# Three small moves in a kernel bound by TensorE: an earlier weight load with a later transpose, later first scores, and one mix on another engine

## Chip, cores, metric

One core of a Trainium2 chip. The metric is the device time of one execution in microseconds (us); medians of several executions are quoted. All comparisons are between fast-state runs, except where a run is called slow.

## The reference, cut to what matters

```python
# attention without softmax: 8 batches, 3008 rows, 256 columns, z has 64 columns
scores = (1 / S) * z @ z.T
attn   = maximum(scores, 0) ** 2
x      = u * (attn @ v)
# then for all 24064 rows, with w_in 256x2048 and w_out 2048x256
h   = x @ w_in
out = (h * cos(h)) @ w_out
```

## The kernel before: the parts that matter here

The work is cut into 48 columns of 512 rows (448 in the last column of each batch). Column s has a phase A (value matmuls, with scores for later columns in between) and a phase B (products with `w_in` and, two columns later, with `w_out`). From column 1 on the product with `w_out` is done from sums of parts ("mixes"), for which four mixed weights (`w_mix`) are made once. The order of every engine's instructions is the order in which the code emits them. GpSimd issues the loads that change type; SyncE issues the transposes, which are DMAs too.

To read the traces: matmul results land in PSUM, used here as pairs of banks E (scores, products with `w_in`) and single banks M. ScalarE takes a score's relu into r and the cosine into c. VectorE squares r into A, makes g = h * cos(h) and the sums sm of the value matmuls, and the later mixes s2 and s4. GpSimd makes s1, the early mixes. x is the sums times uT, the transposed u; the code calls that transpose the "turn" of u. A tiles are transposed too, and are written again when they are free.

```python
upool = pool("u", 2)                      # TWO buffers for u, shared by all columns

def load_u(s):                            # issued on GpSimd's queue
    t = upool.tile([P, 4, D], FP16, name="u16")
    load_rows(t, u, s // NC, s % NC)
    u16s[s] = t

def turn_u(s):                            # a transposing DMA, issued on SyncE's queue
    t = upool.tile([P, 8, P], FP16, name="uT")
    nc.sync.dma_start_transpose(t, u16s.pop(s).rearrange("p j d -> p (j d)"))
    uTs[s] = t

def phase_a_first(s, n, extra={}):        # phase A of columns 0, 1 and 2
    # ... (n scores spread over steps lo..hi)
    for i in range(n):
        p = lo + (hi - lo) * i // (n - 1)
        at[p] = at.get(p, 0) + 1
    for i, (dh, k) in enumerate(steps):
        # ... (two value matmuls, "a pair", per step)
        if dh > 0 and (k % 4 == 3):
            drop_piece((b, J, k // 4))
            if s > 0:
                emit_turns((0, 0), 1)     # one A transpose
                if k < 4:
                    turn_u(s)
                elif k < 8:
                    for d in range(2):
                        gate_mul(s - 1, d, late_sums.pop(0))
        for _ in range(at.get(i, 0)):
            emit_score(later=squares if s == 0 and i == lo else None)
    # ...
    hold(late_sums[0][0:1, 0:1])          # GpSimd waits here for the column's sums
    load_u(s + 1)

def mix_early(m, j):                      # on GpSimd
    # ...
    nc.gpsimd.tensor_tensor(s1[:, f, 0:n], g[:, f, low], g[:, lower, low], ALU.add)
    nc.gpsimd.tensor_tensor(g[:, f, low], g[:, f, up], g[:, f, low], ALU.subtract)

# main sequence
phase_a_first(1, 12)
nc.gpsimd.dma_start(w_out16, moe_w_out.rearrange("(k p) f -> p k f", p=P))
for i in range(2):
    emit_h(0, i)()
phase_a_first(2, 14)                      # ends with load_u(3)
emit_turns((0, 3))
turn_u(3)
load_u(4)                                 # GpSimd: the fifth u
load_z(1, 0)
mix_weights()                             # GpSimd: the four mixed weights
phase_b(2)                                # GpSimd: x of column 2, then the first mixes
```

Of the kernel before, what the change touches and what calls it, by code (L numbers as in the profile page):

```python
# [14 lines left out]
def kernel(  # L15
# [9 lines left out]
    nc = tc.nc  # L25
    AF = mybir.ActivationFunctionType
    ALU = mybir.AluOpType
# [4 lines left out]
    P = 128  # L32
# [6 lines left out]
    NSLOT = B * NC  # L39
# [26 lines left out]
    w_out16 = kpool.tile([P, NFT, D], FP16, name="w_out16")  # L66
    w_mix = kpool.tile([P, 4, NFT // 2, P], FP16, name="w_mix")
    s1, s2, s4 = (kpool.tile([P, NFT // 2, 2 * P], FP16, name=n) for n in ("s1", "s2", "s4"))
# [25 lines left out]
    def drop_piece(key):  # L94
        i = pieces.pop(key)
        if pending.get(i):
            pending[i] = "dropped"
        else:
            free_pieces.append(i)
# [46 lines left out]
    def load_rows(t, src, b, g):  # L146
        full = 4 if g < NC - 1 else 3
        nc.gpsimd.dma_start(
            t[:, 0:full, :],
            group_rows(src[b], g),  # L150
        )
        if full == 3:
            for r in range(2):
                nc.gpsimd.dma_start(t[r * H:(r + 1) * H, 3, :], src[b, S - H:S, :])
# [6 lines left out]
    def load_u(s):  # L161
# [4 lines that stand above are left out]
    def turn_u(s):  # L166
# [3 lines that stand above are left out]
# [64 lines left out]
    def emit_turns(due, more=0):  # L234
        while turns and (turns[0][0] <= due or more > 0):
            if turns[0][0] > due:
                more -= 1
            (b, c), key = turns.pop(0)
            b, J, I = key
            i = turn_slots[key]  # L240
            a = piece_bufs[i]
            if I == J:
                a4 = a.rearrange("p (k w) -> p k w", w=CW)
                for rr in range(1, 4):
                    rows = P if J * 4 + rr < NB - 1 else H
                    nc.sync.dma_start_transpose(
                        a4[:, 0:rr, rr * P:rr * P + rows],
                        a[0:rows, rr * CW:rr * CW + rr * P],
                    )
            else:  # L250
                d = new_piece((b, I, J))
                nc.sync.dma_start_transpose(d.rearrange("p (n j) -> p n j", j=P), a)
            if pending.pop(i) == "dropped":
                free_pieces.append(i)
# [10 lines left out]
    def emit_value(b, J, k, t, dh, bank, start, stop):  # L265
        nc.tensor.matmul(  # L266
            bank[:, 0:width(J)],
            vs[b, k // 4][t * H:(t + 1) * H, k % 4, dh * P:(dh + 1) * P],
            value_rhs(b, J, k, t),
            start=start,  # L270
            stop=stop,
        )
# [8 lines left out]
    def gate_mul(s, dh, sm, eng=None):  # L281
        eng = eng or nc.vector
        J = s % NC
        b = s // NC
        W = width(J)
        if s not in xs:
            if J == NC - 1 and b % 2 == 1:
                xs[s] = xodd
            else:
                xs[s] = xpool.tile([P, 2, CW], FP16, name="x")  # L290
        x = xs[s]
        uT = uTs[s].rearrange("p (k d) j -> p k d j", d=2)
        nk = W // P
        eng.tensor_tensor(  # L294
            x[:, dh, 0:nk * P].rearrange("p (k j) -> p k j", j=P),
            sm[:, 0:nk * P].rearrange("p (k j) -> p k j", j=P),
            uT[:, 0:nk, dh, :],
            ALU.mult,
        )
        if nk < 4:  # L300
            dst = x[:, dh, nk * P:W] if b % 2 == 1 else xodd[:, dh, W:CW]
            eng.tensor_tensor(
                dst, sm[:, nk * P:W], uT[:, nk, dh, 0:W - nk * P], ALU.mult
            )
# [47 lines left out]
    def hold(src):  # L352
        nc.gpsimd.tensor_copy(mark[:, 0:1], src)

    def phase_a_first(s, n, extra={}):
        b, J = s // NC, s % NC
        ea = e_order.pop(0)
        pair = [E[ea][:, 0, :], E[ea][:, 1, :]]
        acc = [pair, M] if s == 1 else [M, pair]
        last = NB - 1  # L360
        run = 1 if s == 0 else 2
        steps = [
            (dh, k)
            for I in range(0, NC, run)
            for dh in range(2)
            for k in range(4 * I, min(4 * (I + run), last))
        ] + [(2, last)]
        lo, hi = 5 if s == 0 else 2, 42
        at = {}
        for i in range(n):  # L370
            p = lo + (hi - lo) * i // (n - 1)
            at[p] = at.get(p, 0) + 1
        for i, (dh, k) in enumerate(steps):
            if i in extra:
                extra[i]()
            if dh == 2:
                emit_value(b, J, last, 0, 0, acc[0][0], False, True)
                emit_value(b, J, last, 1, 1, acc[1][1], False, True)
            else:
                for t in range(2):  # L380
                    emit_value(
                        b, J, k, t, dh, acc[dh][t], k == 0, k == last - 1 and t != dh
                    )
            if dh > 0 and (k % 4 == 3):
                drop_piece((b, J, k // 4))
                if s > 0:
                    emit_turns((0, 0), 1)
                    if k < 4:
                        turn_u(s)
                    elif k < 8:  # L390
                        for d in range(2):
                            gate_mul(s - 1, d, late_sums.pop(0))
            for _ in range(at.get(i, 0)):
                emit_score(later=squares if s == 0 and i == lo else None)
        if s == 0:
            turn_u(0)
        late_sums.extend(gate_sum(s, *acc[dh]) for dh in range(2))
        hold(late_sums[0][0:1, 0:1])
        load_u(s + 1)
        e_order.append(ea)  # L400

# [31 lines left out]
    def halves_of(m):  # L433
        n = T if mwidth(m) == CW else P
        return n, slice(0, n), slice(T, T + n)

    def mix_early(m, j):
        g, f = gs[m], slice(2 * j, 2 * j + 2)
        n, up, low = halves_of(m)
        lower = slice(F + 2 * j, F + 2 * j + 2)  # L440
        nc.gpsimd.tensor_tensor(s1[:, f, 0:n], g[:, f, low], g[:, lower, low], ALU.add)  # L441
        nc.gpsimd.tensor_tensor(g[:, f, low], g[:, f, up], g[:, f, low], ALU.subtract)  # L442

    def mix_late(m, which, c):
        g, f = gs[m], slice(4 * c, 4 * c + 4)
# [146 lines left out]
    def phase_b(s):  # L592
        y, hs = s - 2, [(s - 1, i) for i in (0, 4, 1, 5, 2, 6, 3, 7)]
        if s == 2:
            hs = [(0, i) for i in range(2, 8)] + hs
        for dh in range(len(late_sums)):
            gate_mul(s, 2 - len(late_sums), late_sums.pop(0), nc.gpsimd)
        if mixed(y):
            late = s == NSLOT
            ys = [  # L600
                lambda n=n, i=i: product(y, n, i)
                for i, n in enumerate((1, 5) + order_y[2:] if late else order_y)
            ]
            if mwidth(y) < CW:
                ys.insert(4, lambda: middle(y))
        else:
            ys = [lambda i=i: emit_y(y, i) for i in range(8)]
            ys[7] = lambda f=ys[7]: (f(), store_y(y))
        n = len(hs)
        if n > 8:  # L610
            after = (1, 2, 4, 5, 7, 8, 10, 11)
        elif s == NSLOT:
            after = (0, 1, 3, 4, 5, 6, 7)
        elif mixed(y):
            after = (0, 1, 2, 3, 4, 5, 6, 6)
        else:
            after = (0, 1, 2, 3, 4, 5, 6, 6)
        for i, (m, unit) in enumerate(hs):
            times_c = emit_h(m, unit)
            if not mixed(y):  # L620
                times_c()
            for f, place in zip(ys, after):
                if place == i:
                    f()
            if mixed(y):
                times_c()
            if s == NSLOT and i in (1, 3):
                for c in range(2):
                    mix_late(y, "s2" if i == 1 else "s4", c)
            if mixed(m) and unit >= 4:  # L630
                mix_early(m, unit - 4)
            if i in (1, 3, 5):
                emit_turns((0, 0), 1)

# [4 lines left out]
    for g in range(NC):  # L639
        eng = nc.sync if g % 2 == 0 else nc.scalar  # L640
# [77 lines left out]

    phase_a_first(0, 12, {4: lambda: turn_late(4), 8: lambda: turn_late(5)})
    phase_a_first(1, 12)  # L720
    nc.gpsimd.dma_start(w_out16, moe_w_out.rearrange("(k p) f -> p k f", p=P))
    for i in range(2):
        emit_h(0, i)()
    phase_a_first(2, 14)
# [65 lines left out]
```

## Time and profile before

| | before |
|---|---|
| median of 5 runs | 1192.74 us (1192.59 to 1193.79) |
| span in the profile | 1191.2 us |
| TensorE busy | 1183.7 us (99%) |
| GpSimd busy | 679.0 us (57%) |

How to read the profile: a row of the timeline gives start, duration, engine, line, operation, output<-input, how many instructions were merged (x16) and, in brackets, how long the engine had stood idle before it and what ended that. The lines that carry the argument are shown in the prediction below.

### The profile page before, as it was taken

How to read it: one execution, taken by the hardware profiler on the slowest of the kernel's cores; microseconds unless marked ns; L12 is line 12 of the kernel's file. 1: busy time of each engine (PE TensorE's matmuls, PEld its weight loads, DVE VectorE, ACT ScalarE, POOL GpSimd, SP SyncE). 2: the span in 40 equal slices, each digit the busy share in tenths (PEclk: the TensorE clock that was granted, in tenths of full speed). 3: DMA queues.
4: the chain of work that ended last, by engine and by line, in shares of the span. 5: the costliest groups of instructions: out<-in, count | busy, mean ns of one | idle time of the engine just before them, and what ended most of it. 6: DMA issues, size and time to landing. Idle time of an engine off the chain costs nothing.

```text
span 1191.2 us, 29044 instructions
## 1 busy us (share of the span) xinstructions
PE 1183.7 (99%) x11887; PEld 726.8 (61%) x11887; DVE 1011.5 (85%) x1302; ACT 794.9 (67%) x927; POOL 679.0 (57%) x717
## 2 busy tenths in 40 slices
PE   9999999999999999999999999999999999999998
PEld 4556665665566656666566665656666566665566
DVE  6888888889988898888988889888888888888776
ACT  7966676667666676667676676666766666666454
POOL 3286745657466573755647556476555655545452
PEclk9999999999999999999999999999999999999999
DMA  9999999569995799955999469984798837974301
GB/s 160 175 172 158 115 171 130 102 122 104 173 127 101 123 137 166 126 89 103 155 152 130 86 106 158 168 123 70 120 162 152 122 72 120 173 122 84 65 20 54
DMA packets 449142, 148.00 MB, mean 124 GB/s; under 512 B 401264, under 2 KB 432496, under 8 KB 449008
## 3 DMA queue, kind: packets, MB, share of 16 engines
q1 hardware_dynamic: 368464, 112.93, 56.6%
q0 software_dynamic: 80032, 32.78, 27.7%
q8 instruction: 93, 1.52, 0.5%
q10 hardware_dynamic: 512, 0.43, 0.1%
q14 instruction: 41, 0.34, 0.1%
HBM read 66.32 MB, written 24.64 MB: 76 GB/s over the span
## 4 chain that ended last, share of the span: by engine, by line
PE 98%; ACT 1%; DVE 1%; issue 0%; POOL 0%; DVEq 0%; ACTq 0%
PE E L412 27%; PE M L490 23%; PE M L266 20%; PE E L266 19%; PE E L202 6%; PE M L533 1%; ACT r L212 1%; PE M L468 1%; DVE g L423 0%; PE E L673 0%; DVE sm L278 0%; PE E L533 0%; POOL s L441 0%; PE M L696 0%; ACT c L420 0%
## 5 line engine op out<-in xcount | busy, mean ns | idle before, releaser
L420 ACT ACTIVATE c<-E 128x1024 f16<-128x1024 f32 (+1 forms) x384 | 385.7, 1007 | 216.4 <-PE E L412 214.1
L423 DVE SCALAR_TENSOR_TENSOR g<-E,c 128x1024 f16<-128x1024 f32 (+1 forms) x384 | 458.9, 1197 | 62.0 <-ACT c L420 60.9
L212 ACT ACTIVATE r<-E 128x512 f16<-128x512 f32 (+1 forms) x342 | 328.0, 967 | 112.3 <-PE E L202 106.6
L266 PEld LDWEIGHTS <-v 64*128 64x128 f16 x4512 | 245.7, 94 | 229.6 <-issue 18.8
L412 PE MATMUL E<-x,w_in 128*128 128x512 f16 (+1 forms) x1408 | 354.0, 375 | 0.0
L441 POOL TENSOR_TENSOR s<-g 128x512 f16<-128x512 f16 (+1 forms) x184 | 207.8, 1130 | 189.3 <-DVE g L423 139.4
L266 PE MATMUL M<-A,v 64*128 64x512 f16 (+1 forms) x2256 | 283.0, 372 | 0.0
L266 PE MATMUL E<-A,v 64*128 64x512 f16 (+1 forms) x2256 | 278.0, 371 | 0.0
L442 POOL TENSOR_TENSOR g<-g 128x512 f16<-128x512 f16 (+1 forms) x184 | 219.0, 1190 | 14.4
L412 PEld LDWEIGHTS <-w_in 128*128 128x128 f16 x1536 | 133.1, 98 | 108.9 <-issue 19.5
L490 PEld LDWEIGHTS <-g 128*128 128x128 f16 x2816 | 172.5, 98 | 40.8
L217 DVE TENSOR_TENSOR A<-r 128x1024 f16<-128x1024 f16 x240 | 173.2, 734 | 15.1 <-ACT r L212 14.3
L294 POOL TENSOR_TENSOR x<-sm,uT 128x512 f16<-128x512 f32 (+1 forms) x43 | 48.6, 1131 | 223.5 <-DVE sm L278 223.5
L490 PEld LDWEIGHTS <-s 128*128 128x128 f16 x2112 | 129.4, 98 | 32.1 <-DVE s L448 0.5
L202 PE MATMUL E<-zT 64*128 64x512 f16 (+4 forms) x684 | 128.0, 356 | 1.6 <-DVE sm L278 0.7
L448 DVE TENSOR_TENSOR s<-s,g 128x1024 f16<-128x1024 f16 (+1 forms) x92 | 99.7, 1085 | 2.1 <-POOL s L441 2.1
L490 PE MATMUL M<-w_mix,s 128*128 128x128 f16 x1408 | 94.0, 219 | 0.3 <-POOL s L441 0.3
L490 PE MATMUL M<-w_mix,g 128*128 128x128 f16 x1408 | 93.6, 219 | 0.0
L490 PE MATMUL M<-w_out,g 128*128 128x128 f16 x1408 | 93.6, 219 | 0.0
L220 DVE TENSOR_TENSOR A<-r 128x512 f16<-128x512 f16 (+1 forms) x102 | 80.1, 785 | 8.6 <-ACT r L212 7.6
L202 PEld LDWEIGHTS <-zT 64*128 64x128 f16 x684 | 38.7, 94 | 38.4 <-issue 3.8
L450 DVE TENSOR_TENSOR s<-g,s 128x1024 f16<-128x1024 f16 (+1 forms) x92 | 60.6, 661 | 0.0
(58 smaller groups left out, 636.3 us busy)
## 6 DMA issues: line engine op xcount, KB each, us to landing
out_dram<-o SPq DMA_DIRECT2D x87, 256.0 KB, 2.1
v<-in_v_dram POOLq DMA_DIRECT2D x40, 256.0 KB, 11.5
u<-in_u_dram POOLq DMA_DIRECT2D x40, 256.0 KB, 4.5
A<-A SPq DMA_TRANSPOSE x252, 5.3
z<-in_z_dram POOLq DMA_DIRECT2D x14, 192.0 KB, 10.9
z<-in_z_dram POOLq DMA_DIRECT2D x14, 176.0 KB, 6.8
v<-in_v_dram POOLq DMA_DIRECT2D x8, 192.0 KB, 16.1
u<-in_u_dram POOLq DMA_DIRECT2D x8, 192.0 KB, 3.7
```

The costliest lines, as they stand in the source:

```text
L202: nc.tensor.matmul(e[:, t, 0:Wt], zT[rows, k * P:(k + 1) * P], zT[rows, J * CW:J * CW + Wt], start=True, stop=True,)
L212: nc.scalar.activation(r[:, :, 0:W], e[:, :, 0:W], AF.Relu)
L217: nc.vector.tensor_tensor(a4, r4, r4, ALU.mult)
L220: nc.vector.tensor_tensor(a4, r[:, :, 0:W], r[:, :, 0:W], ALU.mult)
L266: nc.tensor.matmul(bank[:, 0:width(J)], vs[b, k // 4][t * H:(t + 1) * H, k % 4, dh * P:(dh + 1) * P], value_rhs(b, J, k, t), start=start, ...
L412: nc.tensor.matmul(e[:, f, 0:W], w_in16[:, k, ft * P:(ft + 1) * P], x[:, k, 0:W], start=(k == 0), stop=(k == 1),)
L420: nc.scalar.activation(c[:, :, 0:W], e[:, :, 0:W], AF.Sin, bias=half_pi, scale=inv_s2)
L423: return lambda: nc.vector.scalar_tensor_tensor(gs[m][:, 2 * i:2 * i + 2, 0:W], e[:, :, 0:W], 1.0, c[:, :, 0:W], ALU.mult, ALU.mult)
L441: nc.gpsimd.tensor_tensor(s1[:, f, 0:n], g[:, f, low], g[:, lower, low], ALU.add)
L442: nc.gpsimd.tensor_tensor(g[:, f, low], g[:, f, up], g[:, f, low], ALU.subtract)
L448: nc.vector.tensor_tensor(s2[:, f, 0:n], s1[:, f, 0:n], g[:, f, up], ALU.subtract)
L490: nc.tensor.matmul(acc[:, k * P:(k + 1) * P], left[:, ft, k * P:(k + 1) * P], right[:, ft, :], start=(ft == 0 and k == 0), stop=(ft == F - ...
```

## The change

Intent: have `w_out` on the chip in good time, so that the scores can be moved back without TensorE then waiting for it; start the first scores of columns 1 and 2 only when their PSUM pair is free; take away TensorE's wait for the very last early mix by doing it on the faster VectorE.

```diff
@@ phase_a_first
             p = lo + (hi - lo) * i // (n - 1)
+            if s > 0 and i < 2:
+                p = (2, 8)[i] if s == 1 else (5, 9)[i]
@@
-                    if k < 4:
+                    if k // 4 == (0 if s == 1 else 3):
                         turn_u(s)
-                    elif k < 8:
+                    elif 4 <= k < 8:
@@
         hold(late_sums[0][0:1, 0:1])
+        if s == 1:
+            nc.gpsimd.dma_start(w_out16, moe_w_out.rearrange("(k p) f -> p k f", p=P))
         load_u(s + 1)
@@
-    def mix_early(m, j):
+    def mix_early(m, j, eng=None):
+        eng = eng or nc.gpsimd
@@ (its two instructions)
-        nc.gpsimd.tensor_tensor(...)
+        eng.tensor_tensor(...)
@@ phase_b
-                mix_early(m, unit - 4)
+                last_pair = m == NSLOT - 2 and unit == 7
+                mix_early(m, unit - 4, nc.vector if last_pair else None)
@@ main sequence
     phase_a_first(1, 12)
-    nc.gpsimd.dma_start(w_out16, moe_w_out.rearrange("(k p) f -> p k f", p=P))
```

More of the change, by code (lines that the diff above doesn't have):

```diff
@@ L387, in phase_a_first @@
                     emit_turns((0, 0), 1)
-                    if k < 4:
+                    if k // 4 == (0 if s == 1 else 3):
                         turn_u(s)
-                    elif k < 8:
+                    if 4 <= k < 8:
                         for d in range(2):
@@ L440, in mix_early @@
         lower = slice(F + 2 * j, F + 2 * j + 2)
-        nc.gpsimd.tensor_tensor(s1[:, f, 0:n], g[:, f, low], g[:, lower, low], ALU.add)
-        nc.gpsimd.tensor_tensor(g[:, f, low], g[:, f, up], g[:, f, low], ALU.subtract)
+        eng.tensor_tensor(s1[:, f, 0:n], g[:, f, low], g[:, lower, low], ALU.add)
+        eng.tensor_tensor(g[:, f, low], g[:, f, up], g[:, f, low], ALU.subtract)
     def mix_late(m, which, c):
```

## The prediction

> **What bounds the kernel now.** I read the page first: busy shares, then the 40 slices, then the chain that ended last.
>
> ```profile
> span 1191.2 us, 29044 instructions
> PE 1183.7 (99%) x11887; PEld 726.8 (61%) x11887; DVE 1011.5 (85%) x1302; ACT 794.9 (67%) x927; POOL 679.0 (57%) x717
> PE   9999999999999999999999999999999999999998
> PE 98%; ACT 1%; DVE 1%; issue 0%; POOL 0%; DVEq 0%; ACTq 0%
> ```
>
> TensorE is the bound almost everywhere: 1183.7 of 1191.2 us, and 98% of the chain. The change removes no matmul, no activation and no elementwise work, so it can only win what TensorE stands still: 7.5 us by this count. Busy time hides part of a stall, because a matmul's row runs some 0.17 us beyond the start of the next, so I took the timeline of TensorE and compared the start of each row with the start of the next at the pace that its undisturbed rows keep: 0.216 us for one 512-column matmul of 128 rows, or for a pair of 64-row ones (a score of two and four value pairs: 25.07 to 26.15, five times 0.216). What lies above that is a true stall. The sum of them: about 4 us in the first 13 us (loads, first transposes; untouched by the change), about 2.6 us between 23 and 53 us, then nothing above 0.3 us at one place until 1168, 0.5 us at 1169 and 0.2 us at 1172, and after the last matmul some 4 us of eviction and store, untouched too. The change aims at exactly the two stretches in the middle of this list. The waits of the stretch from 14 to 60 us and of the last 36 us name them:
>
> ```profile
> PE E L202 <- DVE sm L278: 0.7, 1, 0.7
> PE E L202 <- DVE g L423: 0.4, 1, 0.4
> PE M L490 <- POOL s L441: 0.3, 1, 0.3
> ```
>
> These are the only sizeable TensorE waits left after the first transposes. The timeline shows where they stand. First TensorE at the start of columns 1 and 2 (the columns that the code calls s = 1 and s = 2), then ScalarE and VectorE around them:
>
> ```profile
> 23.58 0.83 PE L266 MATMUL E<-A,v 64*128 64x512 f16 x6
> 25.07 0.39 PE L202 MATMUL E<-zT 64*128 64x512 f16 x2 [0.66 <-DVE sm L278]
> ...
> 38.24 1.22 PE L266 MATMUL M<-A,v 64*128 64x512 f16 x6
> 39.88 0.39 PE L202 MATMUL E<-zT 64*128 64x512 f16 x2 [0.42 <-DVE g L423]
> 40.09 0.82 PE L266 MATMUL M<-A,v 64*128 64x512 f16 x6
> 41.01 0.39 PE L202 MATMUL E<-zT 64*128 64x512 f16 x2
> ```
> ```profile
> 25.50 11.17 ACT L212 ACTIVATE r<-E 128x1024 f16<-128x1024 f32 x11 [0.51 <-PE E L202]
> 40.30 12.84 ACT L212 ACTIVATE r<-E 128x1024 f16<-128x1024 f32 x14 [0.82 <-PE E L202]
> 38.60 2.36 DVE L423 SCALAR_TENSOR_TENSOR g<-E,c 128x1024 f16<-128x1024 f32 x2
> ```
>
> Six value matmuls from 23.58 should end at 24.23; the next score starts at 25.07: 0.85 us lost. Six from 38.24 should end at 38.89; the score starts at 39.88: 1.0 us lost (0.4 of it is an M bank that the sum of column 1 still reads, the rest the score's E pair, which the first g reads to 39.8). From 40.09 six end at 40.74, the next score starts at 41.01: 0.28 us, the second g. Note ScalarE: it has few pauses in both columns, which decides the first gain below. And the end:
>
> ```profile
> 1168.44 1.16 POOL L441 TENSOR_TENSOR s<-g 128x512 f16<-128x512 f16 x1 [0.82 <-DVE g L423]
> 1169.65 0.40 PE L490 MATMUL M<-w_mix,s 128*128 128x128 f16 x4 [0.32 <-POOL s L441]
> 1169.76 1.23 DVE L423 SCALAR_TENSOR_TENSOR g<-E,c 128x1024 f16<-128x1024 f32 x1 [0.26 <-ACT c L420]
> 1170.90 1.28 DVE L448 TENSOR_TENSOR s<-s,g 128x1024 f16<-128x1024 f16 x2
> 1171.64 0.83 PE L490 MATMUL M<-w_mix,s 128*128 128x128 f16 x9
> 1172.23 0.11 PEld L490 LDWEIGHTS <-s 128*128 128x128 f16 x2 [0.15 <-DVE s L448]
> ```
>
> The fourth quarter of product 5 waits for the last early mix on GpSimd, 0.5 us. Two microseconds later product 6 waits for the two s2 halves on VectorE, and VectorE is 2.00 of 2.00 us busy in every 2 us from 1170 to 1180.
>
> **What the Trainium skill says.** "Perfetto Trace Analysis", Optimization Strategy: find the gaps on the binding engine and the instruction that releases them. That is the method above, and this trace agrees that hardly any gaps are left. "VectorE: DVE Perf Modes", Mode 2×_1P: packed 16-bit tensor-tensor work gives two results per cycle; 512 columns at the page's 0.96 GHz are an estimated 0.27 us plus a fixed part. The trace: 418 ns for the 128x512 form of L450, and 0.60 us from start to start of two 1024-column forms. "GPSIMD Engine Reference", Specifications: GpSimd shares its SBUF interface with VectorE instructions that read two SBUF inputs. The trace agrees: L448 of the same kind takes from 686 ns (median) to 1645 ns, yet 0.68 us at 1170.90, late in a GpSimd row. "DMA: Bandwidth & Descriptors", Queues, rings and completion order: an engine takes queue rows in turn, packet by packet, so moving w_out ahead of u2 within one queue helps w_out, but transposes on the other queue still take their turns. Here the DMA engines show 9 in nearly every slice from 36 to 55 us.
>
> **Part 1, first scores of column 1** (second score from step 5 to step 8; the first stays). The E pair is free at 25.02 as before, so this score still starts at 25.07, but three more value pairs (3 x 0.216 = 0.65 us) are done by then. ScalarE is the check. The relus can follow each other every 0.93 us (two c in 1.96 us, one 1.02); they now come every 1.01 us (11.17 us for eleven), because TensorE paces them. A score may start when the relu two before it has ended, as there are two E pairs to alternate between. Stepping through: relu 2 starts at 25.50 as before; score 3 at 25.50 instead of 26.15; score 4 wants 26.36, but relu 2 ends at 26.52, so it starts at 26.55 instead of 27.01 (0.19 of the gain lost); from there all starts are 0.46 earlier, to the last score at 34.75 instead of 35.21 and its relu at 35.18 instead of 35.64. So ScalarE catches up by the same 0.46, and so do the sums, the two c and the two g behind it. Gain 0.46 us for every engine, not 0.85.
>
> **Part 2, first scores of column 2** (steps 2 and 5 to 5 and 9; with the third at 8 the real order is 5, 8, 9, 11). M bank free at 38.19 instead of 38.65; step 5 is reached at 39.49, the first g ends at 39.33, so no wait: 39.49 instead of 39.88. The second score comes at 40.55 (second g), the third at 40.98, with three more pairs done than before. But ScalarE decides: relu 2 starts at 40.98 (before 41.44), and from it the relus run at 0.93 without a pause; score 4 waits 0.4 us for relu 2, scores 5 to 10 for the relu two before. Already before, scores 9 and 10 waited so (0.06 and 0.22 us). At the last score I get 51.24 instead of 51.63. So part 2 moves a wait from the column's start to its middle and adds nothing: the two columns together are worth about 0.4 us.
>
> **Part 3, w_out and u2.** w_out is issued at some 38.1 instead of 39.09 and no longer behind 256 KB of u2; it landed 14.4 us after its issue, at 53.5, and its first use is at 54.62 (from now on 54.2). So it was hidden by 1.1 us and stays hidden, by about 3. The turn of u2 sat at 49.38 for 4.04 us in a transpose queue that is served one after the other to 72 us; it swaps places with three A transposes and ends near 66, and x of column 2 needs it on GpSimd near 67. Worth 0, close to a small wait off the path.
>
> **Part 4, last mix on VectorE.** GpSimd loses 1.16 + 1.16 us. VectorE gains two 512-column instructions, 0.33 us each from start to start (0.60 less half of 0.53): 0.66. They stand between g(46,7), ending 1168.36, and g(47,0). Gain: product 5 has its last quarter by 1168.7, so the 0.5 us wait goes and TensorE reaches product 6 at 1171.1. Cost: g(47,0) moves from 1168.27 to 1168.93, g(47,1) from 1169.76 to 1170.06 (0.26 us of idle time absorbs the rest), the s2 halves end at 1171.8 and 1172.47 instead of 1171.54 and 1172.18. Product 6 was already waiting for exactly these, so its second half starts 0.3 us later than before. The wait moves, grows, and the end comes 0.3 us later.
>
> **Sum:** -0.4 + 0 + 0 + 0.3 = -0.1 us.
>
> **Rivals.** (a) The stalls are simply won: 0.65 + 0.65 + 0.5, some 1.8 us, 1190.9. For it: the waits shown by name are these. Against: the ScalarE rows without pauses and product 6's wait. (b) The front wins 0.4 to 0.9 us because the relus have more room than 0.93 lets them, and VectorE's two additions are hidden: 1191.9 to 1192.2. For it: the 0.26 us of idle time, and GpSimd off the shared interface. (c) The columns lose all: u2's transpose or w_out lands late under the extra A transposes, or VectorE's queue at 100% delays the last g: up to 1193.2. For it: DMA engines are full; against: 1 us and more of room. A difference of 2% would be 24 us, three times all the idle time of TensorE.
>
> **Range and chances.** The steps give 1192.6; rival (b) is likelier than (c), which pulls to 1192.5. Runs of the kernel before lie 0.3 us apart. Eight in ten: 1191.7 to 1193.2. Chances: faster 0.005, same 0.99, slower 0.005.
>
> **What would show it.** Right: the waits on sm and g at the scores of columns 1 and 2 nearly gone, but scores of column 2 starting one relu after another with small waits, phase B of the third column (52.88) beginning 0.3 to 0.6 us earlier; no wait on L441 at 1169, a larger one for the s2 halves; VectorE without idle time from 1167. Wrong: 52.88 earlier by 1 us or more (relus closer than 0.93), or product 6 not later in distance from the end, or a wait on w_out near 54.

## More of the kernel before

```profile
56.03 0.53 POOL L148 DMA_DIRECT2D u<-in_u_dram  x1 [0.44 <-issue]
58.61 2.14 POOL L459 TENSOR_TENSOR w_mix<-w_out 128x1024 f16<-128x1024 f16 x1
```

The load goes out without waiting for anything, and the mixes follow.

## The result

| | before | changed |
|---|---|---|
| median of 5 runs | 1192.74 us (1192.59 to 1193.79) | 1203.95 us (1202.58 to 1205.7) |
| span in the profile | 1191.2 us | 1202.4 us |
| TensorE's mean granted clock | 1.000 | 0.996 |

The ratio is 1.0093 (95% interval 1.0078 to 1.0107), some 11 us slower. Ratios are the mean time of one kernel's fast runs over that of the other's of the same rounds, so not quite the ratio of the medians quoted. I had predicted 1192.5 us with a range from 1191.7 to 1193.2. The change is within 2%, as forecast, but the time is far outside the range.

The page of the changed kernel: span, TensorE, its busy tenths in 40 slices, its granted clock in the same slices (9 stands for 90% or more of full speed), and the chain that ended last (the work followed back from the last instruction, at each step to what released it).

```profile
span 1202.4 us, 29044 instructions
PE 1188.5 (99%) x11887; PEld 729.0 (61%) x11887; DVE 1011.9 (84%) x1304; ACT 794.5 (66%) x927; POOL 677.0 (56%) x715
PEclk9998999999999999999999999999999999999999
PE 94%; POOL 2%; DVE 2%; ACT 1%; DMA 0%; issue 0%; SPq 0%; ACTq 0%; POOLq 0%
```

Busy shares say next to nothing: TensorE is again at 99%. Two things do: the clock row has an 8 in the fourth slice (90 to 120 us), where before it was 9 throughout, and the chain now contains 2% of GpSimd, some 24 us, where it had none.

To find the place I compared the starts of the same TensorE rows in both traces:

| TensorE row | before | changed | lateness gained since the row above |
|---|---|---|---|
| a score near 20 us (not touched by the change) | 20.56 | 20.29 | -0.27 |
| first product with w_in after column 2 | 52.88 | 52.16 | -0.45 |
| first value matmul of column 3 | 72.06 | 72.88 | +1.54 |
| first product after column 3 | 83.28 | 87.24 | +3.14 |
| first product of the last column | 1165.88 | 1176.52 | +6.68 |
| last product with w_out | 1184.96 | 1196.16 | +0.56 |

So the scores won their 0.45 us, the tail lost 0.56, and between 52 and some 100 us about 11.4 us went. The rest of the kernel, over 1000 us, is the same. The waits of the changed kernel from 14 to 104 us (engine, line, waited for, us in total, times, longest):

```profile
POOL u L148 <- DMA uT<-u: 10.6, 1, 10.6
DVE s L453 <- POOL s L446: 9.8, 2, 7.7
ACT r L212 <- DVE A L220: 5.4, 1, 5.4
PE M L538 <- DVE sm L278: 1.4, 1, 1.4
```

Each of these is absent before. The first stands in GpSimd's queue, in front of everything else. The chain that ended last, in order of time, read for the stretch from 54 to 105 us (start, us, what):

```profile
62.23 4.49 DMA uT<-u
...
67.28 0.53 POOL u L148
67.81 2.03 POOL z L127 x2
...
72.07 6.47 POOL w_mix L464 x3
78.54 2.23 POOL x L294 x2
80.76 1.12 POOL s L446
...
90.21 0.04 DVE s L453
```

Here is the whole story in order. The transpose of the third u is issued at 62.23 (before: 49.38) and lands at 66.72. Only then may GpSimd issue its load of the fifth u, at 67.28 instead of 56.03. Behind it in the same queue stand the loads of z, the four mixed weights, x of column 2 and the first mixes, each now some 11.3 us later (first mix at 80.72 instead of 69.30). VectorE, also in order, waits 7.7 us for the second addition among them (its s2 needs two), with a square behind it in its queue; ScalarE waits 5.4 us for that square to free its buffer; TensorE waits for ScalarE. x of column 2 reads the same late transpose, but that landed at 66.72, before the start that x had in the kernel before (67.07): here it is the load that was held up, and x only behind it. TensorE's timeline:

```profile
82.25 1.92 PE L266 MATMUL E<-A,v 64*128 64x512 f16 x16
87.24 1.89 PE L416 MATMUL E<-x,w_in 128*128 128x512 f16 x4 [3.07 <-ACT r L212]
...
95.79 1.07 PE L416 MATMUL E<-x,w_in 128*128 128x512 f16 x4 [1.97 <-DVE sm L278]
...
98.36 1.87 PE L416 MATMUL E<-x,w_in 128*128 128x512 f16 x4
```

The four matmuls of 1.03 us in an undisturbed row take 1.89 and 1.87 us after the pauses: the clock is at half there. The windows view gives the granted clock as 0.50 from 87 to 91 us and 1.00 from 80 to 84.

### The profile page after: what moved, and what is told of

Its sections match the earlier page's. It is cut to its first block, busy times and chain, and to the rows that moved or that the text cites. A ratio compares the mean times of both kernels' runs of the same rounds, so it can differ in the third digit from the quotient of the medians.

```text
span 1202.4 us, 29044 instructions
## 1 busy us (share of the span) xinstructions
PE 1188.5 (99%) x11887; PEld 729.0 (61%) x11887; DVE 1011.9 (84%) x1304; ACT 794.5 (66%) x927; POOL 677.0 (56%) x715
## 4 chain that ended last, share of the span: by engine, by line
PE 94%; POOL 2%; DVE 2%; ACT 1%; DMA 0%; issue 0%; SPq 0%; ACTq 0%; POOLq 0%
PE E L416 26%; PE M L495 23%; PE M L266 20%; PE E L266 19%; PE E L202 5%; ACT r L212 1%; POOL w_mix L464 1%; PE M L473 1%; DVE g L427 1%; PE M L538 0%; POOL s L446 0%; DMA uT<-u 0%; POOL g L447 0%; PE E L679 0%; DVE A L217 0%
## 5 line engine op out<-in xcount | busy, mean ns | idle before, releaser
L447 POOL TENSOR_TENSOR g<-g 128x512 f16<-128x512 f16 (+1 forms) x183 | 218.5, 1194 | 14.3
```

What stands on the lines that cost most here:

```text
L447: eng.tensor_tensor(g[:, f, low], g[:, f, up], g[:, f, low], ALU.subtract)
```

## The experiments

Theory U: the fifth u needs the buffer of the third u (the pool has two), the late transpose keeps that buffer, and the load of the fifth u, waiting in GpSimd's in-order queue, holds up all that stands behind it. Rival W: `w_out` ahead of the third u starves the A transposes, those starve the squares, and this carries on; the wait in GpSimd's queue would be a companion. Besides, the three other parts are measured alone.

Kernels are compared only within the same rounds. Chips differ in scatter (on one the kernel before ran from 1193.08 to 1197.31), so for effects under 2 us I rely on starts of rows in the trace. These scatter too: between the first product after column 3 and the last column two runs (mix alone, w_out alone) lost 0.72 us that no part of their edit accounts for, so small effects are read between nearby rows only. A table of the starts stands at the end of this section.

### The turn put back

```diff
-                    if k // 4 == (0 if s == 1 else 3):
+                    if k < 4:
                         turn_u(s)
```

> The changed kernel with the turn of the third u put back to its old place (all else changed). Theory U (the load of the fifth u on GpSimd needs the buffer of the third u, whose transpose now comes late, and holds GpSimd's queue in order for 10.6 us): GpSimd's wait for the uT transpose falls from 10.6 us to under 4, which the queue's slack of some 2.4 us mostly absorbs; no 3 us stall of TensorE at 84 us, clock 1.00; 1193 to 1195 us (front gain 0.7, a 1.5 us stall at 54 us from w_out, tail +0.6). Rival W (w_out ahead of u2 starves the A transposes, which starve the squares, and that carries on): it stays at 1201 or more.

Measured: 1195.54 us (before 1194.59), ratio 1.0014 (0.9993 to 1.0035). GpSimd's load of the fifth u in this run:

```profile
57.07 0.53 POOL L148 DMA_DIRECT2D u<-in_u_dram  x1 [0.62 <-DMA uT<-u]
```

It waits 0.62 us instead of 10.57, the stall of 3 us and the low clock are gone, and almost all of the loss with them: the last product starts 1.12 us later than in the kernel before, not 11.2. The median lies 0.5 us above the range that I expected. Theory U holds, with `w_out` early all the time.

### The late turn alone

```diff
# in the kernel before, only:
-                    if k < 4:
+                    if k // 4 == (0 if s == 1 else 3):
                         turn_u(s)
```

> The kernel before with only the late turn of the third u (u2 still loaded ahead of w_out, old scores, old mix). Theory U: the full loss comes back alone, GpSimd's load of the fifth u waits some 10 us, 1201 to 1204 us. Rival W: without the w_out move there is no loss, 1192.5 to 1194 us.

Measured: 1202.52 us (before 1194.59), ratio 1.0069 (1.0048 to 1.0091).

```profile
67.45 0.53 POOL L148 DMA_DIRECT2D u<-in_u_dram  x1 [11.86 <-DMA uT<-u]
```

The u was loaded ahead of `w_out` here, as before the change, and the loss comes back nearly whole: the last product of the trace starts at 1195.40, 10.4 us late. From column 3 to the last column it loses 9.5 us, where the changed kernel loses 9.8. Rival W had allowed 1192.5 to 1194 us and falls as the explanation of the 11 us. The rest is a wait of TensorE for `w_out` (0.9 us), which landed 16.4 us after its issue instead of 14.4. Whether the missing turn of u did that is not shown: three runs that share the early code of the kernel before (itself, order alone, mix alone) had 14.4, 14.6 and 15.6.

### The wait moved behind the weight mixes

```diff
-    load_u(4)
     load_z(1, 0)
     mix_weights()
+    load_u(4)
```

> The changed kernel, but GpSimd issues the load of the fifth u after the four weight mixes instead of before them, so that its wait no longer stands in front of them; the turn stays late and w_out stays early. Theory U: weight mixes at about 58 to 67 us again, TensorE without the stall at 84 us and at clock 1.00, 1193 to 1195 us. Rival W: no effect, 1203 to 1205 us.

Measured: 1196.73 us (before 1194.59), ratio 1.0015 (0.9996 to 1.0034). The turn is still late, yet 7.4 us are back by the start of the last product (1188.77 against 1196.16 in the changed kernel): the mixed weights are made at 57 to 66 us again. What is left comes from the late turn too:

```profile
71.92 0.59 POOL L148 DMA_DIRECT2D u<-in_u_dram  x1 [6.24 <-DMA uT<-u]
72.53 2.29 POOL L294 TENSOR_TENSOR x<-sm,uT 128x512 f16<-128x512 f32 x2
```

In this run the turn lands at 71.4 us only (66.7 in the changed kernel; why is open). x of column 2 and the first mixes come 5.5 us late, and TensorE loses 2.6 us at 87. The load stands in front of x, but x reads the transpose itself and would have waited for it as well, so this rest cannot be put down to the load's wait. My range (1193 to 1195) was missed by 1.7 us. A third buffer for u would have been the cleaner trial, but it does not fit: the memory on the chip is short by a few hundred bytes per partition for one pool and by 3 kB for the next. So the buffer itself was not changed in any run; that the buffer is what the load waits for is read from the profile's wait on the transpose and from the code, and that this wait costs the time is shown by these three runs.

### Matmuls of no use while TensorE waits

15 and 16 matmuls into a PSUM bank that the next product overwrites anyway, before the first and third product after column 3. They change no result.

```diff
+        if s == 3:
+            filler_b(15)
...
+            if s == 3 and i == 2:
+                filler_b(16)
             times_c = emit_h(m, unit)
```

> The changed kernel with 15 and 16 matmuls of no use in front of the first and third product of the column where TensorE stands still, so that it never idles for 3 us there. In the changed kernel's records TensorE's clock is 0.5 for some of 86 to 100 us. If the low clock follows from the idle time, the clock stays at 1.00, and since the third product waits for VectorE's chain anyway, only the slow matmuls after it are won back: 1.5 to 2.5 us faster than the changed kernel, 1201.5 to 1202.5 us. If the low clock has another cause, or all of the loss is low clock: no change (1204), or 4 us and more faster.

Measured: 1203.82 us (before on that chip 1194.59), ratio 1.0077 (1.0058 to 1.0096). The window from 86 to 88 us of this run (each engine's busy time, then granted clock, DMA share, GB/s):

```profile
86.00:88.00 2.00, 1.73 (x9) 0.61 (x8) 2.00 (x2) 0.60 (x1) 1.92 (x3) 1.00 0.00 0
```

The clock is 1.00 here, and in every 2 us from 82 to 100, where it was 0.50 for most of 86 to 100. So the low clock follows from the idle time. The Trainium skill says this in "TensorE: Matmul & The Clock Gate", What's actually happening: an idle window of about 3.4 us halves the clock, and about as much busy time restores it. The traces agree in kind, but not in the length. In the changed kernel the pause was 3.07 us, and the granted clock fell between 86.0 and 86.5, some 2 us after the last matmul. It fell again after a pause of 1.97 us (1.00 from 95 to 96, 0.50 from 97 to 100), while a pause of 2.41 us in the run with the load behind the mixes left it at 1.00. It came back at about 93, after some 6 us of work, and at about 100, some 3.4 us after its second fall. So a pause shorter than the page's window can be enough, and its length alone does not decide.

The last product starts 1.15 us earlier than in the changed kernel (1195.01 against 1196.16), although the third product starts 0.51 us later (96.30 against 95.79; GpSimd's first mix was 0.41 us later in this run). So the slow matmuls after 95.79 cost some 1.7 us. Those before lay in time that TensorE would have waited anyway. Of the eleven microseconds some 1.7 are the clock, the rest is waiting. By time alone I had expected 1201.5 to 1202.5 us and missed it.

### The scores alone

```diff
+            if s > 0 and i < 2:
+                p = (2, 8)[i] if s == 1 else (5, 9)[i]
```

> The kernel before with only the later first scores of columns 1 and 2. My steps of the prediction: the first product after column 2 starts at 52.5 instead of 52.88 us. As measured in the changed kernel: 0.5 to 0.7 us earlier. No part of it should be lost later unless the first use of w_out (54.62 before) now meets its landing: 1191.9 to 1192.4 us on a chip that gives 1192.7 for the kernel before.

Measured: 1193.76 us (before 1193.33), ratio 0.9996 (0.9984 to 1.0008). The first product after column 2 starts 0.45 us earlier (52.59, with this run's score near 20 us 0.16 late), as the steps of the prediction said (0.39). Then:

```profile
54.88 1.05 PE L535 MATMUL M<-w_out,g 128*128 128x256 f16 x8 [0.39 <-DMA w_out<-in_moe_w_out_dram]
```

TensorE meets the landing of `w_out` and the gain is gone. The 1191.9 to 1192.4 us that I expected did not come. The slack that I had put at 1.1 us is no constant: in this run `w_out` took 16.0 us from issue to landing, before 14.4, in others up to 17.3. This is the wait that the change wanted to avoid by loading `w_out` earlier.

### The w_out load alone

> The kernel before with only the w_out load ahead of the third u, whose turn keeps its old place. If w_out ahead of the A transposes is what stalls TensorE at 54 us in the changed kernel (a square waits for an A transpose that is in flight with w_out): a square of column 2 waits over 1 us for a DMA of A, TensorE loses 0.5 to 1.5 us near 54, total 0.3 to 1.5 us slower. If that stall came from the late turn or the moved scores: no wait there, within 0.3 us of the kernel before.

The edit is the third and last hunk of the diff above, nothing else. Measured: 1194.79 us (before 1193.33), ratio 1.0011 (0.9997 to 1.0025).

```profile
53.94 1.29 DVE L217 TENSOR_TENSOR A<-r 128x1024 f16<-128x1024 f16 x2 [2.32 <-DMA A<-A]
55.88 0.82 PE L535 MATMUL M<-w_out,g 128*128 128x256 f16 x6 [1.31 <-DVE sm L278]
```

`w_out` is there in time, but now a square waits 2.3 us for an A transpose that is reading its buffer, the sums of column 2 come late and TensorE waits 1.3 us for the bank that they read. This is the stall of the changed kernel at 54 us (1.54 us by its row starts). So rival W is real, with a size of 1 to 1.5 us: it is a second, smaller cost beside theory U. The stall is also there in the changed kernel, where no turn of u stands among these transposes, so it is not that turn that holds them up. That the transposes are slowed by sharing the DMA engines with `w_out` I infer; what is seen is that the one in question is not done when `w_out` is issued ahead of it, and is done in time when `w_out` is issued behind it.

### The mix alone

The edit is the `mix_early` part of the diff. 

> The kernel before with only the last early mix on VectorE. Steps of the prediction: the wait of 0.5 us at 1169 goes, the halves of s2 come 0.3 us later, the end 0.3 us later. From the changed kernel's trace: the two additions take 0.94 us of VectorE, not 0.66, because the first waits for the g before it and the second for the first; the end is 0.5 to 0.6 us later, the wait of product 6 over 1 us. If the move were a gain by itself: the end 0.5 us earlier.

Measured: 1193.67 us (before 1193.33), ratio 1.0004 (0.999 to 1.0019); totals cannot decide this. In the trace, from the first product of the last column to the last product: 19.65 us, before 19.08. The last part of the change costs 0.57 us.

```profile
1169.26 0.43 DVE L442 TENSOR_TENSOR s<-g 128x512 f16<-128x512 f16 x1
1169.72 0.42 DVE L443 TENSOR_TENSOR g<-g 128x512 f16<-128x512 f16 x1
1173.07 1.11 PE L491 MATMUL M<-w_mix,s 128*128 128x128 f16 x14 [0.71 <-DVE s L449]
```

The wait for s1 has gone, and product 6 stands 1.1 us (0.71 of it as idle time) for the halves of s2, exactly as the prediction argued, only longer. The reason is in the first two rows: the addition starts 1.26 us after the g whose result it reads (two g that do not depend on each other start 1.13 us apart, and in the kernel before an s2 that does not read the g in front of it starts 1.14 us after it), and the subtraction 0.46 us after the addition, which reads what it overwrites. The two took 0.94 us of VectorE, not the 0.66 that I had put down.

### Another order of the last products

```diff
-                for i, n in enumerate((1, 5) + order_y[2:] if late else order_y)
+                for i, n in enumerate((1, 2, 5, 6, 7, 3, 4) if late else order_y)
```

Product 2 needs no mix, so it can fill the time in which products 5 and 6 would wait for theirs. First with the scores, then alone:

> A candidate: the kernel before, the later first scores, and at the end, instead of the mix on VectorE, another order of the last products (1, 2, 5, 6, 7, 3, 4), so that products 5 and 6 come 1.75 us later, when the mix on GpSimd and the halves of s2 are done. Expected: no wait of TensorE for s1 or s2 near 1169 and 1172 (0.7 us), with 0.5 to 0.7 us of the scores: 1.0 to 1.5 us faster than the kernel before. It fails if VectorE, full at the end, delays a later product.

Measured: 1193.59 us (before 1193.33), ratio 1.0002 (0.9984 to 1.002). The tail is 18.54 us (before 19.08), without any wait for s1 or s2; the gain of the scores is lost to `w_out` as above, and 0.3 us at 96 us, where TensorE waits for a bank that VectorE still reads. That wait also came up in runs whose early part is untouched, so I count it as scatter. The 1.0 to 1.5 us that I expected did not come.

> The kernel before with only the other order of the last products. From the trace of the run with scores and order: no wait near 1169 and 1172, the end 0.6 to 0.7 us earlier counted from the first h of the last column (1165.88 to the start of the last product at 1184.96, 19.08 us before; 18.4 to 18.5 expected). The total moves less than runs on this chip scatter.

Measured: 1193.03 us (before 1193.1), ratio 0.9997 (0.9984 to 1.001). Every row up to the last column starts where it did before (1165.88), and the last product at 1184.42 instead of 1184.96: 0.54 us, a little less than the 0.6 to 0.7 expected. As a time it cannot be told from the scatter.

### w_out in two halves

```diff
-    nc.gpsimd.dma_start(w_out16, moe_w_out.rearrange("(k p) f -> p k f", p=P))
+    for i in range(2):
+        nc.gpsimd.dma_start(
+            w_out16[:, i * F:(i + 1) * F, :],
+            moe_w_out.rearrange("(k p) f -> p k f", p=P)[:, i * F:(i + 1) * F, :],
+        )
```

> The last candidate (kernel before, later first scores, product order 1, 2, 5, 6, 7, 3, 4) with the w_out load cut in two halves by rows, issued where the kernel before issues it, behind the third u. In the run with the scores alone TensorE waited for w_out at its first use (start 54.88 instead of 52.59 + 1.73 = 54.32), which ate the gain of 0.45 us. The first product needs only the first half; if that wait is what ate it, TensorE starts on w_out 1.73 us after 52.3 to 52.6 with no wait for its DMA, and the end is 1.0 to 1.3 us earlier than before (0.45 + 0.7). If instead the gain is lost to the DMA engines being full (the first half no earlier than the whole was), the wait stays and it is 0.6 to 0.7 us.

Measured: six runs, of which one took 4413.28 us and was the profiled one. In it the matmuls kept about a quarter of their pace from the first microseconds to the last (a score took 0.84 us, where 0.216 is usual), while the granted clock in the records reads 1.000. I do not know why, and nothing is concluded from it. The others gave 1192.64 once and 1196.09 to 1196.84 four times (before 1193.1); ratio 1.0019 (1.0007 to 1.0031).

> The kernel with w_out in two halves once more, because its profiled execution fell into a state 3.7 times as slow, in which every matmul took four times its time, and four of its five other runs gave 1196.1 to 1196.8, one 1192.6. This look is for a trace in the ordinary state. If the 3 us are in this kernel itself: a stall of some 3 us of TensorE that the kernel before has not, somewhere from 54 to 130 us, with the weight mixes (which need the second half) later than 58.6 us. If not: about 1192 us and no wait for w_out at its first use.

Measured: 1193.34 and 1194.09 us (before 1193.02), ratio 1.0001 (0.9983 to 1.002). In this trace TensorE does not wait for `w_out` any more, but 1.26 us at the same place for the sums of column 2, behind a square that starts 2.1 us late. The 3 us are not in this trace; what they were stays open. The split gives nothing: the wait for the load has been turned into one of the same place and size as in the run with `w_out` ahead. That it is the same wait is not shown, because the profile names ScalarE's copy of the sums, not a DMA, as what ended the square's wait here.

### w_out 13 us earlier

```diff
# with the scores and the other order of the last products
         load_u(s + 1)
+        if s == 0:
+            nc.gpsimd.dma_start(w_out16, moe_w_out.rearrange("(k p) f -> p k f", p=P))
```

> Another candidate for the same wait: scores and product order as in the last ones, and w_out in one piece, but issued at the end of column 0 (near 25 us), behind the second u, 13 us before the kernel before issues it. If only the landing of w_out ate the gain of the scores, TensorE starts on w_out without a wait, 0.4 to 0.5 us earlier than before, and the end is 1.0 to 1.3 us earlier. If w_out in flight beside the A transposes of column 1 delays them and the second u's turn as it did in the changed kernel, squares of column 2 or of column 1 wait for a DMA of A and it is 0 to 1.5 us slower than before.

Measured: 1192.24 us (1191.71 to 1192.55) against 1193.02 of the kernel before, ratio 0.9988 (0.9974 to 1.0001). In the trace the first product with `w_out` starts at 54.16 (before 54.62) without a wait, a square waits 0.5 us for a transpose, which costs TensorE nothing, and the last product starts at 1183.96, 1.00 us before its start in the kernel before: 0.46 from the scores, 0.54 from the order. This is the best of all kernels tried. The interval just includes 1.

Starts in us of the rows named in the result section:

| run | near 20 | after col. 2 | column 3 | after col. 3 | last column | last product |
|---|---|---|---|---|---|---|
| before | 20.56 | 52.88 | 72.06 | 83.28 | 1165.88 | 1184.96 |
| changed | 20.29 | 52.16 | 72.88 | 87.24 | 1176.52 | 1196.16 |
| turn put back | 20.56 | 52.43 | 72.62 | 83.84 | 1166.44 | 1186.08 |
| late turn alone | 20.56 | 52.88 | 72.96 | 87.41 | 1176.32 | 1195.40 |
| load behind the mixes | 20.56 | 52.43 | 72.61 | 83.84 | 1169.13 | 1188.77 |
| fillers | 20.34 | 52.21 | 72.73 | 87.64 | 1175.37 | 1195.01 |
| scores alone | 20.72 | 52.59 | 72.34 | 83.56 | 1166.16 | 1185.24 |
| mix alone | 20.56 | 52.89 | 72.19 | 83.42 | 1166.74 | 1186.39 |
| w_out alone | 20.14 | 52.46 | 73.11 | 84.33 | 1167.65 | 1186.73 |
| scores and order | 20.44 | 52.31 | 72.05 | 83.28 | 1166.20 | 1184.74 |
| order alone | 20.56 | 52.88 | 72.06 | 83.29 | 1165.88 | 1184.42 |
| w_out in halves, again | 20.34 | 52.20 | 72.63 | 83.86 | 1166.60 | 1185.14 |
| w_out earlier | 20.56 | 52.42 | 71.60 | 82.83 | 1165.42 | 1183.96 |

## Why the prediction was wrong, point by point

- **Bound, and what can be won.** Right. TensorE bounds the kernel, little idle time could be won, and the three places named were the three places.
- **Parts 1 and 2, the scores.** Right in mechanism and nearly in size: 0.4 us said, 0.45 found in the changed kernel and in the run of the scores alone. The recurrence over E pairs and relus predicted that the two moves together would be worth 0.4 and not 1.3 us, and the small waits in the middle of column 2 are there.
- **Part 3, w_out and u2.** This is the step that failed: "it swaps places with three A transposes and ends near 66, and x of column 2 needs it on GpSimd near 67. Worth 0, close to a small wait off the path." The transpose did end near there (66.72). But I asked only who reads what the transpose writes. I did not ask who needs the buffer that it reads. With two buffers the fifth u takes the third's, and its load is issued at 56 us on GpSimd's queue. The Trainium skill has the rule that makes this costly, in "DMA: Bandwidth & Descriptors", Anatomy of one DMA: DMA engines do not wait on semaphores; the wait takes place on the issuing sequencer before dispatch. This trace agrees: GpSimd stood still for 10.57 us, with the weight mixes ready behind the load (`w_out` had landed at 52.3). The lateness of 11.3 us in GpSimd's queue reached TensorE as 9.8 us, about 8 of waiting and 1.7 of low clock.
- **Part 3, the slack of w_out.** Also wrong in size: 1.1 us of slack was read from one landing. From issue to landing `w_out` took 14.2 to 17.3 us in the runs that issued it whole near 38 us, and in the changed kernel the slack was 1.6 us, not the 3 that I had put down. And moving it ahead cost 1.0 to 1.5 us through the A transposes, which the sum had put at 0 and no rival had named: rival (c) let the A transposes delay `w_out` and u2, not the reverse.
- **Part 4, the last mix.** Right in direction and mechanism against the obvious reading: the wait moves to product 6 and grows. The term of the sum that was mis-sized is the two instructions on VectorE, 0.66 us said, 0.94 measured, because each waits for the one in front; the end is 0.56 us later instead of 0.3.
- **Rivals and range.** Rival (c) had "u2's transpose lands late", but as something that touches TensorE through x, limited to 1193.2. The range was made from the terms I had, with no room for a wait that I had not looked for. The changed order of the transposes was in front of me, and with it a later end for one buffer.

The sum in the end, from the row starts: -0.27 (start, scatter), -0.45 (scores), +1.54 (w_out and the A transposes), +9.8 (fifth u behind the late turn, with the clock), +0.56 (mix) = +11.2 us.

## What to carry to other kernels

When a transfer is moved later, follow both ends of it: who reads what it writes, and who is waiting to overwrite what it reads. In an in-order queue the second one stops everything behind it, so a load that may wait for a buffer belongs behind the work that is urgent, not in front of it. And taking a wait away from a bound engine by loading an engine that is full a moment later only moves the wait; reordering independent work into the gap (product 2 here) removed it.

## What the Trainium skill lacked or had wrong

- "VectorE: DVE Perf Modes", The DRAIN you can't avoid, says from a trial of copies that a semaphore between two instructions costs nothing extra. It gives no cost for an instruction that depends on the one in front, and the views here do not show whether a semaphore stands between the two. Here an instruction that reads the result of the one in front started 1.26 us after a g of 1.23 us, where an independent g started after 1.13; and a subtraction that overwrites an input of the addition in front of it started 0.46 us after it, while the g that follows it came 0.34 us after. Dependence cost about 0.12 us per pair.
- "TensorE: Matmul & The Clock Gate", Seeing it yourself, mentions a clock stuck at a quarter for over 50 us. One execution here ran all of its 4411.5 us with matmuls at about a quarter of their pace, and the granted clock in its records was 1.000. Whether it is the same state is open. As to the window under What's actually happening: the pauses after which the clock was halved here (3.07 and 1.97 us) were shorter than it.
- No page that I read says how far a load's landing scatters when transposes run beside it: 1 MB of `w_out` (cast while loading) took 12.3 us when issued at 25 us; 14.4, 14.6 and 15.6 in three runs that issue it as the kernel before does; and 14.7, 14.5 and 17.3 in three with the changed kernel's code up to that point.
